# Dealing the 8 KB runs of a KV cache to the SBUF partitions in another order

## The chip, the cores and the metric

One core of one Trainium2 chip runs the kernel. The metric is the device time of one launch in microseconds (us). The core has five instruction queues: TensorE (PE, with its weight loads shown as PEld), VectorE (DVE), ScalarE (ACT), GpSimd (POOL) and SyncE (SP). SP computes nothing here; it issues nearly all transfers between DRAM and the on-chip memory SBUF, which has 128 partitions. 16 DMA engines carry the transfers out in packets; one packet is one contiguous run.

## The reference

One decode step of an attention block and a gated MLP side by side on the same normalised input, and the gradient of it for all inputs but one. All data are bf16.

```python
xn = _layernorm(x)                                   # x: [2, 1, 576]
q = (xn @ wq).reshape(B, Sq, 32, 128)                # 32 query heads, 16 KV heads
scores = einsum("bhqd,bhkd->bhqk", q, k) * 128**-0.5 # k_cache, v_cache: [2, 16, 4096, 128]
o = einsum("bhqk,bhkd->bhqd", softmax(scores), v)
out = x + o.reshape(B, Sq, 4096) @ wo + ((xn @ w_gate) * (xn @ w_up)) @ w_down
_out, _vjp = jax.vjp(_f, A_x, A_k_cache, A_v_cache, A_wq, A_wo, B_w_gate, B_w_up, B_w_down)
_grads = _vjp(grad_out)
```

The outputs are `out` and the gradients of `x`, both caches (each as large as the cache, 32 MB), `wq`, `wo` and the three MLP weights. There is one query position, so a cache is read once, and its gradient is an outer product that is written once. The sum over the 4096 keys doesn't depend on the order of the keys, as long as K, V and their gradients use the same order.

## The kernel before

The function is one long builder. Python generators (`load_kv`, `turn`, `softmax`, `dscore`, `contract`, `head_outer`, `put` and others) yield requests, and a planner (`Order`, lines 105 to 240) runs them against a table of costs and priorities and so writes down one fixed order of instructions for each engine. Nothing is scheduled on the chip: SP issues its transfers in the order written, and each waits for the semaphores of its data or buffer. The planner lets at most eight transfers of the hardware queue be in flight: an issue waits for the landing of the one eight places before it (line 186).

The work is cut into 16 steps: 8 groups of two KV heads, times 2 batch entries. For each step and each of the two heads:

- `load_kv` (lines 1108 to 1121) loads one K head and later one V head, 4096 x 128 elements or 1 MB each, into one of the 16 shared `big` tiles (128 partitions x 4096 elements). The load is issued at line 1117: `nc.sync.dma_start(kv_t[i][:], views[t][b, G * g + l])`. There are 64 such loads.
- `turn` (line 1175) transposes 32 x 32 blocks on DVE (the helper at line 464) into another `big` tile, and `score` (line 1228) multiplies on PE (line 1234). `softmax` and `dscore` follow.
- `contract` (line 1390) uses the loaded tile itself for the weighted sum over the keys (line 1407).
- `head_outer` (line 1244) forms the gradient of a K or V head with PE (line 1255), ACT or DVE copy it from PSUM into a `big` tile (helpers at lines 468 and 470), and `put` (lines 687 to 692) stores it through `oviews`. The store's issue is line 691. There are 64 such stores of 1 MB.

A head's 4096 keys lie in DRAM as 1 MB without a gap. `views` and `oviews` (lines 1105 and 1106) tell which keys go to which partition: partition p holds the 32 keys from 32p on, an 8 KB run. All code between load and store treats the position within a tile as the key's name, and nothing in it uses the key's place in DRAM.

Beside that, `load_w` (line 1123) brings the weights, `group_front`, `group_back` and `mlp` work on them, and the weight gradients leave through `put` too: `rows_outer` with 4,608-byte rows, `cols_store` and `wide_outer` with rows of 1 to 4 KB over 128 partitions, and `tail_outer` (line 808), which stores 64 rows of 1 KB from 64 partitions of a `tl` tile.

Of the kernel before, what the change touches and what calls it, by code (L numbers as in the profile page):

```python
# [13 lines left out]
P = 128  # L14
# [339 lines left out]
def kernel(  # L354
# [747 lines left out]
    wS = [[None] * 2 for _ in range(NS)]  # L1102
    bE = [[Event() for _ in range(2)] for _ in range(NS)]
    bS = [[None] * 2 for _ in range(NS)]
    views = [A.rearrange("b h (p c) d -> b h p (c d)", p=P) for A in (A_k_cache, A_v_cache)]
    oviews = [A.rearrange("b h (p c) d -> b h p (c d)", p=P) for A in (out_2, out_3)]

    def load_kv():
        n = 0
# [449 lines left out]
```

## Time and profile before

| | us |
|---|---|
| median of three runs | 478.5 (477.12 to 479.41) |
| the profiled execution | 480.7 |
| its span, first to last instruction | 478.9 |
| DVE busy | 369.2 |
| PE busy | 375.8 |
| ACT busy | 335.6 |

The profiled execution is one run; its span leaves 1.8 us of start and end around it. Each engine's busy time is a share of that span. A line of the profile such as "L691" is a line of the code. "out_dram<-big" is a store from a `big` tile, "big<-in_A_k_cache_dram" a load. The row of DMA tenths has 40 slices of 12 us, each with the mean busy share of the 16 DMA engines. The queue line gives packets, megabytes, and the time of the packets as a share of 16 engines' span. The chain is the work that ended last, followed back from the last instruction. A wait line tells who waited, for whom, and the total in us, the times and the longest. The granted clock of TensorE was 0.704 in the mean.

### The profile page before, as it was taken

What the parts mean: (1) busy time and instruction counts of PE and PEld (TensorE: products, weight loads), DVE (VectorE), ACT (ScalarE), POOL (GpSimd) and SP (SyncE); (2) the same over time, 40 slices, a digit from 0 to 9 for tenths busy, and PEclk for the clock granted to TensorE, in tenths of its full rate; (3) what the DMA queues carried; (4) which work ended last, traced back from release to release, by engine and by line L of the source; (5) the groups of instructions that cost most, each with busy time, mean ns of one, the idle gap of its engine ahead of it and who ended that gap; (6) DMA issues with size and microseconds to landing.
All of it is one profiled execution on the core that took longest, in us unless ns stands there. A gap on an engine that the chain in (4) does not pass through costs nothing.

```text
span 478.9 us, 15380 instructions
## 1 busy us (share of the span) xinstructions
PE 375.8 (78%) x6538; PEld 214.9 (45%) x6538; DVE 369.2 (77%) x708; ACT 335.6 (70%) x507; POOL 152.0 (32%) x208
## 2 busy tenths in 40 slices
PE   1668588989878877768878986599887769898894
PEld 1545353545554534446344453464444424444452
DVE  8788787867867976786956987889677958888781
ACT  3139659966787693833869875399776978897871
POOL 0440074343003643003434530032644556333000
PEclk9979676556766677885567595859656876656876
DMA  8999999999999999999999999999999999999994
GB/s 299 355 405 419 391 402 380 353 377 422 422 400 371 395 365 393 423 414 389 316 399 384 354 402 422 421 413 406 346 414 415 418 419 422 419 417 391 425 369 187
DMA packets 41925, 185.95 MB, mean 388 GB/s; under 512 B 3960, under 2 KB 13440, under 8 KB 25472
## 3 DMA queue, kind: packets, MB, share of 16 engines
q1 hardware_dynamic: 41848, 184.96, 98.3%
q8 instruction: 51, 0.84, 0.7%
q14 instruction: 18, 0.15, 0.1%
q10 hardware_dynamic: 8, 0.00, 0.0%
HBM read 92.48 MB, written 92.48 MB: 386 GB/s over the span
## 4 chain that ended last, share of the span: by engine, by line
DMA 46%; PE 25%; DVE 14%; ACT 8%; issue 3%; SPq 2%; POOL 1%; DVEq 0%; ACTq 0%; POOLq 0%
DMA out_dram<-big 18%; DMA big<-in_A_v_cache_dram 15%; DVE big L464 8%; ACT big L468 7%; PE ps_o L1255 4%; DMA big<-in_A_k_cache_dram 4%; PE ps_m L1234 4%; PE ps_m L1407 4%; PE ps_o L722 3%; DMA gu<-in_B_w_up_dram 3%; DMA ww<-in_A_wo_dram 3%; DMA big<-in_B_w_gate_dram 2%; DVE big L470 2%; PE ps_m L678 1%; PE ps_o L759 1%
## 5 line engine op out<-in xcount | busy, mean ns | idle before, releaser
L468 ACT CAST big<-ps_o 128x1024 bf16<-128x1024 f32 (+2 forms) x310 | 277.6, 958 | 47.6 <-PE ps_o L1255 18.9
L464 DVE STREAM_TRANSPOSE big<-big 128x1024 f32<-128x1024 f32 x146 | 175.9, 1224 | 29.7 <-DMA out_dram<-big 16.2
L1222 POOL TENSOR_TENSOR BD<-vr,mask 128x2048 bf16<-128x2048 bf16 x32 | 115.3, 3603 | 105.4 <-ACT vr L468 49.8
L470 DVE CAST big<-ps_o 128x1024 bf16<-128x1024 f32 (+2 forms) x68 | 74.2, 1093 | 16.4 <-PE ps_o L722 7.4
L1234 PE MATMUL ps_m<-big,W 128*32 128x128 bf16 x2048 | 59.9, 282 | 11.3 <-DVE cr L1359 2.6
L1234 PEld LDWEIGHTS <-W 128*32 128x32 bf16 x2048 | 46.7, 125 | 27.9 <-issue 25.7
L1255 PE MATMUL ps_o<-BD,dd 32*128 32x512 bf16 x256 | 45.8, 480 | 9.9 <-ACT big L468 7.9
L671 POOL COPY wt<-wm 64x128 bf16<-64x128 bf16 (+1 forms) x34 | 8.9, 261 | 138.2 <-DVE wm L664 119.5
L1255 PE MATMUL ps_o<-BD,pp 32*128 32x512 bf16 x256 | 48.2, 520 | 5.5 <-ACT big L468 4.0
L1199 POOL COPY W<-rep 32x16 bf16<-32x16 bf16 x128 | 24.5, 192 | 55.8 <-DVE rep L983 33.6
L464 DVE STREAM_TRANSPOSE big<-ww 128x1152 f32<-128x1152 f32 x25 | 34.0, 1359 | 7.7 <-DMA ww<-in_B_w_down_dram 3.5
L1407 PE MATMUL ps_m<-big,pp 128*32 128x512 bf16 x256 | 30.2, 547 | 3.8 <-DMA big<-in_A_v_cache_dram 3.3
L1255 PEld LDWEIGHTS <-dd 32*128 32x128 bf16 x256 | 12.2, 98 | 32.1 <-issue 27.6
L1407 PE MATMUL ps_m<-big,dd 128*32 128x512 bf16 x256 | 25.8, 491 | 0.4 <-DVE oT L1427 0.2
L1255 PEld LDWEIGHTS <-pp 32*128 32x128 bf16 x256 | 10.4, 97 | 28.1 <-issue 24.2
L872 PE MATMUL ps_m<-big,Wdy 128*128 128x128 bf16 x162 | 15.4, 269 | 4.8 <-DVE rz L1320 3.1
L722 PE MATMUL ps_o<-dyr,hb 32*32 32x288 bf16 x288 | 18.0, 382 | 0.2 <-ACT big L468 0.2
L759 PEld LDWEIGHTS <-xnr 32*128 32x128 bf16 x368 | 12.9, 116 | 10.8 <-issue 9.7
L722 PE MATMUL ps_o<-dyr,R 32*32 32x288 bf16 x256 | 16.2, 378 | 1.3 <-ACT big L468 0.9
L872 PEld LDWEIGHTS <-Wdy 128*128 128x128 bf16 x162 | 13.6, 121 | 6.8 <-issue 6.7
L759 PE MATMUL ps_o<-D,xnr 32*128 32x128 bf16 x256 | 13.0, 276 | 3.9 <-issue 2.2
L1308 ACT COPY mr<-m 1x128 f32<-1x128 f32 x16 | 4.7, 295 | 15.8 <-DVE m L1306 15.6
(205 smaller groups left out, 487.3 us busy)
## 6 DMA issues: line engine op xcount, KB each, us to landing
out_dram<-big SPq DMA_DIRECT2D x74, 1024.0 KB, 12.8
big<-in_A_k_cache_dram SPq DMA_DIRECT2D x32, 1024.0 KB, 12.7
big<-in_A_v_cache_dram SPq DMA_DIRECT2D x32, 1024.0 KB, 13.2
out_dram<-big SPq DMA_DIRECT2D x17, 576.0 KB, 10.7
ww<-in_B_w_down_dram SPq DMA_DIRECT2D x9, 576.0 KB, 13.5
ww<-in_A_wo_dram SPq DMA_DIRECT2D x8, 576.0 KB, 7.3
ww<-in_A_wq_dram SPq DMA_DIRECT2D x8, 512.0 KB, 8.0
big<-in_B_w_gate_dram SPq DMA_DIRECT2D x4, 1024.0 KB, 12.3
```

Source lines behind the costliest of these rows:

```text
L464: nc.vector.transpose(out, in_)
L468: nc.scalar.copy(out, in_)
L470: nc.vector.tensor_copy(out=out, in_=in_)
L671: nc.gpsimd.tensor_copy(view(Wt[:], 64 * h, 64, 0, [[dims[-1][1], n], [1, dims[-1][1]]]), view(Wm[:], 64 * h, 64, off, dims))
L722: nc.tensor.matmul(o[32 * q:32 * q + 32, aa, 0:HD2], lhsT=view(t, 32 * q, 32, 2 * A + aa, [[4, 32]]), rhs=dyr[32 * q:32 * q + 32, k * HD2: ...
L759: nc.tensor.matmul(o[:, aa, j * P:(j + 1) * P], lhsT=xnr[32 * a:32 * a + 32, dc * P:(dc + 1) * P], rhs=rhs(a), start=True, stop=True)
L872: nc.tensor.matmul(dh, lhsT=Wdy[:, e, 2 * k:2 * k + P], rhs=view(X[:], 0, P, 64 * k + e, [[D, FC], [2, 32]]), start=(k == 0 and e == 0), s ...
L1199: nc.gpsimd.tensor_copy(view(W_t[t][w][:], 32 * a, 32, 6 + 8 * a, [[G * WW, 4], [WW, G], [1, 2]]), view(rep_t[grp[g]["qs"]][:], 32 * a, 32 ...
L1222: nc.gpsimd.tensor_tensor(BD_t[i][:], view(vr_t[v][:], 0, P, 0, [[0, 16], [1, Dh]]), view(mask16[:], 0, P, 0, [[1, 16], [0, Dh]]), ALU.mult)
L1234: nc.tensor.matmul(sc[32 * cq:32 * cq + 32, :], lhsT=view(W[:], 0, P, (be * G + l) * WW + 6 - 4 * c2 - 2 * l, [[1, 32]]), rhs=view(X[:], 0 ...
L1255: nc.tensor.matmul(o[:, k, :], lhsT=pr2[32 * c4:32 * c4 + 32, :], rhs=BD[32 * c4:32 * c4 + 32, 8 * l + 4 * h2:8 * l + 4 * h2 + 4, :], star ...
L1407: nc.tensor.matmul(ct[32 * j:32 * j + 32, :], lhsT=view(rT, 0, P, 4 * c + 2 * l, [[1, 32]]), rhs=kv_t[kvS[s][t][l]][:, Dh * c:Dh * (c + 4) ...
```

## The change

Two lines change. The 128 runs of 8 KB of a head go to other partitions: before, partition p holds run p; after, partition 8e + j holds run 16j + e, for e from 0 to 15 and j from 0 to 7. Loads and gradient stores use the same rule, so the keys of a head are permuted alike everywhere.

```diff
-    views = [A.rearrange("b h (p c) d -> b h p (c d)", p=P) for A in (A_k_cache, A_v_cache)]
-    oviews = [A.rearrange("b h (p c) d -> b h p (c d)", p=P) for A in (out_2, out_3)]
+    views = [A.rearrange("b h (j e c) d -> b h e j (c d)", e=16, j=8) for A in (A_k_cache, A_v_cache)]
+    oviews = [A.rearrange("b h (j e c) d -> b h e j (c d)", e=16, j=8) for A in (out_2, out_3)]
```

The tile's side of the transfer stays 128 partitions of 8 KB; the DRAM side becomes 16 x 8 runs of 8 KB, with a step of 8 KB between the 16 and of 128 KB between the 8.

## The prediction

> **What bounds the kernel now.** I read the page's totals first, then the DMA queues, then the chain that ended last, then what SyncE (SP) waits for before its issues, and last the trace's single DMA packets. Totals and queues:
>
> ```profile
> span 478.9 us, 15380 instructions
> PE 375.8 (78%) x6538; PEld 214.9 (45%) x6538; DVE 369.2 (77%) x708; ACT 335.6 (70%) x507; POOL 152.0 (32%) x208
> ...
> DMA  8999999999999999999999999999999999999994
> ...
> DMA packets 41925, 185.95 MB, mean 388 GB/s; under 512 B 3960, under 2 KB 13440, under 8 KB 25472
> ...
> q1 hardware_dynamic: 41848, 184.96, 98.3%
> ```
>
> No compute engine is above 78%, but the 16 DMA engines are occupied in 38 of 40 slices, and SP's queue alone takes 98.3% of 16 engines' span. Of 478.9 us about 4 us are left in which an engine had no packet. So a change of packet time goes almost fully into the end, and a few tenths at an issue hardly do. The chain agrees:
>
> ```profile
> DMA 46%; PE 25%; DVE 14%; ACT 8%; issue 3%; SPq 2%; POOL 1%; DVEq 0%; ACTq 0%; POOLq 0%
> DMA out_dram<-big 18%; DMA big<-in_A_v_cache_dram 15%; DVE big L464 8%; ACT big L468 7%; PE ps_o L1255 4%; DMA big<-in_A_k_cache_dram 4%; PE ps_m L1234 4%; PE ps_m L1407 4%; PE ps_o L722 3%; DMA gu<-in_B_w_up_dram 3%; DMA ww<-in_A_wo_dram 3%; DMA big<-in_B_w_gate_dram 2%; DVE big L470 2%; PE ps_m L678 1%; PE ps_o L759 1%
> ```
>
> The DMAs on it are the ones that the change touches: stores from `big` and the two cache loads. The waits of SP's queue (total us, times, longest) and the issues themselves (ns min/median/max):
>
> ```profile
> SPq L691 <- ACT big L468: 82.6, 49, 7.7
> SPq L691 <- DVE big L470: 49.9, 17, 6.8
> SPq L1117 <- DMA out_dram<-big: 31.9, 13, 4.8
> ```
>
> ```profile
> L1117 SPq DMA_DIRECT2D big<-in_A_k_cache_dram x32: 327/372/1742, 0.7 to 404.2; - x32
> ```
>
> ```profile
> L691 SPq DMA_DIRECT2D out_dram<-tl x26: 472/507/1971, 34.3 to 469.6; - x26
> ```
>
> SP has slack: its 249 issues take 150 us in all, and a cache load lands 12.7 to 13.2 us after its issue, five transfers of 2.45 us deep.
>
> **The packets.** The trace holds length and size of each. Exactly 16,384 packets of SP's queue have 8,192 B, and they are the cache runs (64 loads and 64 stores of 128 runs): 1,024 for each engine. Their median is 309 ns, 88% lie at or under 313, the mean is 320.7. At 309 they are 1,024 x 0.309 = 316 us of each engine's 475. The excess of the mean is 1,024 x 11.7 ns = 12.0 us, no more. It sits in a few places. From 280 to 304 us, where cache loads and stores alternate, it is nearly absent (mean 312). From 265.6 to 267.1 us, at the start of a store that follows a store, most engines have two or three packets of 600 to 750 ns:
>
> ```profile
> 280.00:304.00 24.00, 16.58 (x361) 10.23 (x364) 18.78 (x35) 12.68 (x21) 2.50 (x11) 0.79 1.01 423
> 264.00:268.00 4.00, 4.00 (x78) 2.15 (x76) 3.24 (x5) 4.00 (x6) 3.60 (x1) 0.50 1.01 322
> ```
>
> The last two columns are DMA share and GB/s: full both times, at 423 and at 322.
>
> **The change, part by part.** No instruction is added or removed, and the order of every engine is the same; in the built program only the shapes of the 128 cache DMAs change: 128 rows on both sides become 16 x 8 rows on the DRAM side and 128 x 1 on the SBUF side. Bytes, run length and packet count stay. Keys are only permuted, alike in K, V and both gradients. Three terms follow.
>
> *DRAM side.* If the slow 8 KB packets come from where the engines stand in DRAM, the change can win up to all of the excess; bounds 0 and -12.0 us. A new clash is bounded by the SBUF term below. Most packets already run at 309, so I take 0 for the forecast and keep -12.0 for the range.
>
> *Issue.* An issue with a shape of its own for each side isn't in the trace. The nearest rows: 128-row issues 327 ns at least, 64-row ones 471. So 0 to +0.14 us each, x128 = 0 to 18 us of SP time. SP's waits (82.6 + 49.9 + 31.9 us in the three rows) and five transfers of depth hide it. Cover is gone only where the DMA engines run dry, as at 224 to 232 us (share 0.77): a handful of times 0.14 us, under 1 us, and at most 5 us if a dependency chain carries thirty of them. I take 0.
>
> *SBUF side.* The new leading count is 16, one for each engine, so the claim of the change (engine e at run 16j + e) means that engine e moves the eight neighbouring partitions 8e to 8e+7. Is that what it has now? The trace doesn't name partitions, but it shows that it matters which ones the engines hold. The transfers with 64 rows (line 812, `tl`) have 1 KB packets, and 46 ns is such a packet alone. From 228.6 to 230.1 us, when the queue had run dry and the engines were in step, two such stores ran: of 120 packets 44 took 50 ns or less and 60 took 66 to 88, often as twins (two at 228.743 us of 79 each, two at 228.77 of 74, two at 228.823 of 79). In the 1 KB stores from 460 to 469 us, nearly all with 128 rows, 1,043 of 1,080 took 50 or less. Half the partitions, and engines meet in pairs, each at about half pace. The first cache load, with all engines in step from 2.6 to 5.2 us, has 87 of 111 packets at 316 ns or less and one over 500: today's deal of 128 rows gives every engine a place of its own. If 64 partitions hold places for 8 engines, then 128 hold 16, and a different deal can put two engines on one.
>
> Price: bounded below by the row alone, 309 ns, so 0; above by the doubled row. 8 KB packets of exactly 606 ns occur 26 times (twice 309 less one fixed 12), so 1,024 x (606 - 309) = +304 us. Between these the overlap decides. Engines drift: the 16 landings of a cache DMA lie 3.4 us apart from first to last, the first ten within 0.73 us, two taken at random 0.75 us (medians over 128 DMAs). A stay of eight packets is 2.45 us, one of four 1.22. Two engines 0.25 us apart overlap for 0.90 or 0.80 of it, 0.75 apart for 0.69 or 0.39. A DMA lands with its last engine and at most eight are in flight, so the pair that is closest sets the pace; I take 0.80: 0.80 x 304 = +243 us.
>
> [...]
>
> **Sum.** The profiled execution took 480.7 us (span 478.9 and 1.8 around it). 480.7 + 0 + 0 + 243 = 723.7. It was 2.2 above the median of the runs, 478.5, so on the medians 721.5, **722 us**.
>
> **The rivals.** (1) *Faster: the DRAM order works and SBUF doesn't mind.* Place: the starts of stores while engines are in step. Price: of the 12.0 us of excess 9.9 lie in packets over 400 ns, and 2.9 of these in packets over 800 ns, starts after a dry queue; 9.9 - 2.9 = 7.0, and 478.5 - 7.0 = **471.5**. It decides if the cache packets keep 309 ns, that is if engines don't share places. For it: packets of 600 to 750 ns on most engines at once look like one shared target, and 16 neighbouring runs can't be the same one at any lag. Against it: 423 GB/s in the long stretches, with the old order.
>
> (2) *Nothing: the SBUF rows stay with their engines, or don't care, and DRAM doesn't either.* **478.5**, within 2.4. For it: the 309 of most packets looks like the engine's own pace. [...]
>
> (3) *Slightly slower:* the packets stay, but the longer issues (up to 0.14 us) reach the end where the queue is shallow, up to 5 us, or a new order meets in DRAM now and then: **483**.
>
> **How the numbers follow.** Forecast 0.58, because the twins and the clean first load speak for places and the new shape can't keep the old deal and do what it says; (1) 0.21; (2) 0.13; (3) 0.08. This kernel's measurement tells about 0.5% (2.4 us) from no change. So faster 0.21, same 0.13, slower 0.58 + 0.08 = 0.66. The cases lie far apart and both signs hold much. The forecast's own range is 600 (overlap 0.4: 478.5 + 122) to 770 (0.96). For 8 in 10 I must take in (1), (2) and (3): 468 (478.5 less 10.5 of the 12.0) to 770.
>
> **What would show it.** Right: 8 KB packets with a mean near 550 ns and many at 606, the DMA share still at 0.9 or more in nearly all slices at about 250 GB/s, cache DMAs landing some 20 us after issue, every compute engine at about two thirds of its present share, other sizes as before. Wrong for (1): 8 KB mean at 310 to 313 and no group of 600 ns. Wrong for (2): mean 321 as now. Issues of lines 691 and 1117 show the second term: 330 to 370 ns, or 470 and more. The prediction falls if the new deal still gives each engine its own eight partitions of one place, or if the twins of the 64-row stores come from DRAM and not from the partitions.

## The result, and the profile after

The changed kernel takes 574.1 us (median of four runs, 569.7 to 575.0) against 478.1 us (477.1 to 479.4) for the kernel before, measured together: a ratio of 1.199, interval 1.195 to 1.203. That is 96 us more. I had predicted 722 us. The direction was right, and the size was two and a half times too large.

The profiled execution took 575.0 us with a span of 573.2 us. From the totals, the slices and the queues of the changed kernel's page:

```profile
span 573.2 us, 15380 instructions
PE 394.5 (69%) x6538; PEld 222.5 (39%) x6538; DVE 370.8 (65%) x708; ACT 336.9 (59%) x507; POOL 152.4 (27%) x208
...
DMA  8999999999999999999999999999999999998996
GB/s 215 301 225 267 310 263 317 323 234 377 398 364 323 394 296 249 393 357 350 323 265 330 356 304 349 399 319 388 271 321 365 362 353 361 367 372 291 369 369 187
DMA packets 41925, 185.95 MB, mean 324 GB/s; under 512 B 3960, under 2 KB 13440, under 8 KB 25472
...
q1 hardware_dynamic: 41848, 184.96, 99.1%
```

The reader is to see three things. The packets and the bytes are exactly those of before, and the DMA engines are as full as before (99.1% of the span). So the engines don't stand idle longer: the same packets take longer, and the rate falls from 388 to 324 GB/s. The loss is uneven: slices of 215 to 270 GB/s stand beside slices of 390 to 400. The compute engines' busy times change little (DVE 369.2 to 370.8, PE 375.8 to 394.5 at a granted clock of 0.644 in place of 0.704); their shares fall, because the span is longer.

The chain that ended last has moved towards the transfers, from 46% to 67%:

```profile
DMA 67%; PE 15%; DVE 6%; ACT 5%; issue 2%; SPq 2%; POOL 1%; DVEq 0%; ACTq 0%; POOLq 0%
```

In the view of single lines, an issue of a cache load now takes at least 536 ns where it took 327 (columns: ns at least, median and at most, then the start of the first and of the last issue in us):

```profile
L1117 SPq DMA_DIRECT2D big<-in_A_k_cache_dram x32: 536/586/1891, 0.7 to 486.2; - x32
...
L1117 SPq DMA_DIRECT2D big<-in_A_v_cache_dram x32: 536/587/2025, 13.7 to 505.3; - x32
```

A K load lands 17.2 us after its issue (12.7 before). The time and the size of every packet in the trace tell where the 96 us are. Per DMA engine, all packets together took 474.6 us before and 572.1 us after, 97.6 us more:

| packets | mean before | mean after | per engine |
|---|---|---|---|
| 8,192 B, cache loads and stores, 1,024 per engine | 320.7 ns | 399.2 ns | +80.3 us |
| 2,048 B, weight loads, 288 | 100.0 | 121.3 | +6.1 |
| 1,024 B, loads and stores, 528 | 49.7 | 61.2 | +6.0 |
| 4,608 B, loads and stores, 272 | 197.2 | 207.8 | +2.9 |
| 512 B, weight loads, 64 | 27.5 | 42.7 | +1.0 |
| 4,096 B, stores only, 160 | 160.7 | 163.1 | +0.4 |

The median of the 8 KB packets is 309 ns in both kernels. What is new is a second group: about 130 packets took 540 to 640 ns before, about 2,900 after. It isn't there all the time either. In the windows view of the changed kernel (start and end in us, length, busy time of PE, PEld, DVE, ACT and POOL, granted clock, DMA share, GB/s):

```profile
0.00:64.00 64.00, 33.30 (x640) 21.36 (x640) 40.20 (x118) 24.37 (x41) 12.53 (x29) 0.83 0.99 250
136.00:160.00 24.00, 19.33 (x357) 11.71 (x358) 15.46 (x30) 13.36 (x21) 4.18 (x3) 0.67 1.02 407
```

The kernel before, in the same two windows:

```profile
0.00:64.00 64.00, 38.30 (x806) 25.57 (x806) 52.30 (x142) 30.21 (x51) 16.80 (x34) 0.85 0.99 376
136.00:160.00 24.00, 19.93 (x392) 12.46 (x381) 19.15 (x35) 17.61 (x30) 8.35 (x17) 0.64 1.01 388
```

With the same full DMA share, the changed kernel's first 64 us run at 250 GB/s and the 24 us from 136 at 407; the kernel before had 376 and 388. In the first window the cache transfers that land are loads; of the nine that begin to land in the second, six are stores.

### The profile page after: what moved, and what is told of

Its sections match the earlier page's. It is cut to its first block, busy times and chain, and to the rows that moved or that the text cites. A ratio compares the mean times of both kernels' runs of the same rounds, so it can differ in the third digit from the quotient of the medians.

```text
span 573.2 us, 15380 instructions
## 1 busy us (share of the span) xinstructions
PE 394.5 (69%) x6538; PEld 222.5 (39%) x6538; DVE 370.8 (65%) x708; ACT 336.9 (59%) x507; POOL 152.4 (27%) x208
## 3 DMA queue, kind: packets, MB, share of 16 engines
q1 hardware_dynamic: 41848, 184.96, 99.1%
## 4 chain that ended last, share of the span: by engine, by line
DMA 67%; PE 15%; DVE 6%; ACT 5%; issue 2%; SPq 2%; POOL 1%; DVEq 0%; ACTq 0%; POOLq 0%
DMA out_dram<-big 26%; DMA big<-in_A_v_cache_dram 21%; DMA gu<-in_B_w_up_dram 6%; DMA big<-in_A_k_cache_dram 5%; DMA ww<-in_A_wq_dram 4%; ACT big L468 4%; DVE big L464 3%; DMA ww<-in_A_wo_dram 3%; DMA ww<-in_B_w_down_dram 3%; PE ps_m L1234 2%; PE ps_m L1407 2%; PE ps_o L1255 2%; PE ps_o L722 2%; POOL BD L1222 1%; DVE big L470 1%
## 5 line engine op out<-in xcount | busy, mean ns | idle before, releaser
L1234 PE MATMUL ps_m<-big,W 128*32 128x128 bf16 x2048 | 62.8, 290 | 15.9 <-DVE cr L1359 6.1
L1234 PEld LDWEIGHTS <-W 128*32 128x32 bf16 x2048 | 48.5, 128 | 36.3 <-issue 34.7
L1255 PE MATMUL ps_o<-BD,pp 32*128 32x512 bf16 x256 | 49.6, 530 | 8.6 <-ACT big L468 4.2
L1255 PE MATMUL ps_o<-BD,dd 32*128 32x512 bf16 x256 | 47.6, 506 | 9.3 <-ACT big L468 6.9
L1407 PE MATMUL ps_m<-big,dd 128*32 128x512 bf16 x256 | 28.1, 526 | 1.0 <-issue 0.8
L1304 PE MATMUL ps_m<-identf,mx 128*1 128x128 f32 x16 | 5.4, 340 | 25.9 <-DVE mx L1296 25.6
L1255 PEld LDWEIGHTS <-pp 32*128 32x128 bf16 x256 | 10.2, 98 | 31.3 <-issue 27.5
L722 PE MATMUL ps_o<-dyr,R 32*32 32x288 bf16 x256 | 17.2, 401 | 2.0 <-ACT big L468 1.6
## 6 DMA issues: line engine op xcount, KB each, us to landing
big<-in_A_k_cache_dram SPq DMA_DIRECT2D x32, 1024.0 KB, 17.2
```

The source lines that it names most:

```text
L722: nc.tensor.matmul(o[32 * q:32 * q + 32, aa, 0:HD2], lhsT=view(t, 32 * q, 32, 2 * A + aa, [[4, 32]]), rhs=dyr[32 * q:32 * q + 32, k * HD2: ...
L1234: nc.tensor.matmul(sc[32 * cq:32 * cq + 32, :], lhsT=view(W[:], 0, P, (be * G + l) * WW + 6 - 4 * c2 - 2 * l, [[1, 32]]), rhs=view(X[:], 0 ...
L1255: nc.tensor.matmul(o[:, k, :], lhsT=pr2[32 * c4:32 * c4 + 32, :], rhs=BD[32 * c4:32 * c4 + 32, 8 * l + 4 * h2:8 * l + 4 * h2 + 4, :], star ...
L1407: nc.tensor.matmul(ct[32 * j:32 * j + 32, :], lhsT=view(rT, 0, P, 4 * c + 2 * l, [[1, 32]]), rhs=kv_t[kvS[s][t][l]][:, Dh * c:Dh * (c + 4) ...
```

## The experiments

The theory in all of them is that of the prediction: two DMA engines that want the same place in SBUF at the same moment take turns, and the new deal puts them there. It is an inference from times: no trace here names a place. The rivals are the order in DRAM, the longer issues, and a shape that is slow for an engine by itself.

**e1_loads: only the loads are dealt anew.**

```diff
-    views = [A.rearrange("b h (p c) d -> b h p (c d)", p=P) for A in (A_k_cache, A_v_cache)]
+    views = [A.rearrange("b h (j e c) d -> b h e j (c d)", e=16, j=8) for A in (A_k_cache, A_v_cache)]
```

> Only the 64 cache loads get the new deal; the stores keep the old one, so the gradients land in another order of keys. Theory A (places in SBUF: with the new deal an engine moves eight neighbouring partitions, and shares their places with another engine, each direction by itself): about half of the +96 us, 515 to 535 us; 8 KB packets of loads up to 606 ns, those of stores at 309; the weight loads, which write into SBUF too, slower as well, the 64-row stores not. Rival B (the engines meet in DRAM because 16 neighbouring runs are one target): about half as well if reads and writes are alike, but then only one of the two halves if not. Rival C (longer issues, 327 to 536 ns): 64 issues x 0.2 us = 13 us of SP time, nearly all hidden, so under 485 us.

Measured: 574.2 us (572.6 to 577.6), a ratio of 1.199 (1.192 to 1.206), mean of the 8 KB packets 403 ns. That is above the 515 to 535 us that I expected: the loads alone carry the whole loss.

**e2_stores: only the gradient stores are dealt anew** (the `oviews` line of the change, and not the `views` line).

> Only the 64 gradient stores get the new deal; the loads keep the old one, so the gradients land in another order of keys. Theory A: the other half, 515 to 535 us; 8 KB packets of stores up to 606 ns, loads of all sizes as before (512 B packets at 27 ns, 8 KB loads at 309). Rival B: as for the loads. Rival C: under 485 us.

Measured: 500.0 us (498.7 to 503.8), a ratio of 1.046 (1.039 to 1.053), mean of the 8 KB packets 335.8 ns, which is +15.5 us per engine of +17.1 for all packets. That is below the 515 to 535 us expected: stores cost something, a fifth of what loads cost, and beside the dealt loads it doesn't add up. Two causes were possible, the issues and the packets. The issue row of this kernel is nearly as long as that of the full change (343/552 ns at least and in the median, against 344/576; 332/344 before):

```profile
L691 SPq DMA_DIRECT2D out_dram<-big x96: 343/552/2276, 32.4 to 486.7; - x96
```

**e4_issue: the issues alone.** One line at the start of the kernel before turns a switch of the build off:

```diff
+    nc.dge_precook = False
```

> The kernel before with one switch of the build changed, so that every DMA issue of SP is expected to take the long way (470 to 540 ns where a 128-row issue took 327); all transfers, their shapes and their order stay. It asks where the 21 us of the stores-only kernel come from. Theory 'issue' (SP's 0.2 us more per store reach the end): this kernel, in which 249 issues are longer and not 64, is slower by as much or more, 495 to 510 us. Theory 'packets' (the stores' own packets, or what they do to the packets beside them): 478 to 483 us, mean of the 8 KB packets 321 ns as before.

Measured: 478.6 us against 478.3, a ratio of 1.0015 (0.9998 to 1.0032), mean of the 8 KB packets 318.8 ns. The issues did get longer:

```profile
L1117 SPq DMA_DIRECT2D big<-in_A_k_cache_dram x32: 471/552/1279, 0.7 to 401.2; - x32
...
L691 SPq DMA_DIRECT2D out_dram<-big x96: 471/504/3550, 32.7 to 467.4; - x96
```

Some 0.14 us more on each of the 128 issues of these two rows, and on the 32 of the V loads (472 ns at least), costs nothing that can be measured. In the stores-only kernel 64 issues grew by 0.21 us, less in all. So I put its 21 us down to the packets: they hold 17.1 of the 18.0 us by which the profiled span grew (478.9 to 496.9 us).

**m1_forms: the forms by themselves.** A kernel of transfers only, no two of which need each other: `run("load", form, 14)` and `run("store", form, 14)` for the old rows, the new deal, and a third form with the new shape but its 16 leading rows 80 KB apart in DRAM; then loads in two halves of 64 partitions.

```python
if form == "rows":
    return x.rearrange("(p c) d -> p (c d)", p=P)
if form == "deal":
    return x.rearrange("(j e c) d -> e j (c d)", e=16, j=8)
x = x.rearrange("(p c) d -> p (c d)", p=P)
return bass.AP(x.tensor, x.offset, [[40960, 16], [4096, 8], [1, 4096]])
```

> Transfers alone, no computing; of the outputs only part of one cache gradient is written, with cache data. Each stage starts when the one before has landed: 14 loads in the old deal, 14 in the new one, 14 in the shape of the new one but with each engine's eight runs contiguous in DRAM and the engines 80 KB apart; then 14 stores of each kind; then 10 heads loaded as two transfers of 64 rows. One transfer of 1 MB takes 2.45 us at 309 ns a packet. Theory A: old deal 309 ns, 34 to 37 us for the stage; new deal and the 80 KB form alike, 606 ns at the start of the stage, when the engines are in step, 45 to 70 us for the stage; the same for stores; the halves 500 to 606 ns. Rival B: the 80 KB form at 309 like the old deal, only the new deal slow, and the halves at 309.

The windows of this kernel, one inside each stage and two in the stage of dealt stores (the last two columns are DMA share and GB/s; only POOL is named, and it does nothing):

```profile
4.00:36.00 32.00, 0.00 (x0) 1.00 1.01 423
44.00:104.00 60.00, 0.00 (x0) 1.00 1.01 219
112.00:172.00 60.00, 0.00 (x0) 1.00 1.01 225
179.00:207.00 28.00, 0.00 (x0) 1.00 1.01 419
211.00:215.00 4.00, 0.00 (x0) 1.00 0.99 250
222.00:244.00 22.00, 0.00 (x0) 1.00 1.01 419
...
290.00:330.00 40.00, 0.00 (x0) 1.00 1.02 217
```

Loads: old deal 423 GB/s, new deal 219 (packets of 604 ns), new shape with another DRAM order 225, and halves of 64 partitions, whose DRAM order is the old one, 217. The other order in DRAM is worth 3% here (225 against 219); the halving comes without the new order (217) and stays with the other one (225). Stores: old 419, and the new deal 250 for some microseconds and then 419. The third form's stores, in a window left out here, ran at 420 GB/s. So my "each direction by itself" doesn't hold evenly: stores were slow only at their start and recovered by themselves; loads didn't in 60 us.

**e5_near and e6_wide: the same loss without the change, and its absence with the same issues.** The kernel before, each cache load issued as two transfers of 64 partitions, first of neighbours, then of every second partition (of the second kernel only the inner line is shown):

```diff
-                    nc.sync.dma_start(kv_t[i][:], views[t][b, G * g + l])
+                    for h in range(2):
+                        nc.sync.dma_start(kv_t[i][64 * h:64 * h + 64, :], views[t][b, G * g + l][64 * h:64 * h + 64, :])
```

```diff
+                        nc.sync.dma_start(kv_t[i][h:P:2, :], views[t][b, G * g + l][h:P:2, :])
```

> The kernel before, all of it computed, with each cache load issued as two transfers of 64 neighbouring partitions; rows, partitions, DRAM addresses and the number of packets stay as they were, stores too. Theory 'places in SBUF': loads meet in pairs as in the changed kernel, 540 to 590 us, mean of the 8 KB packets 380 to 410 ns. Rival 'order in DRAM': nothing has changed there, 478 to 485 us (64 more issues of 0.47 us), mean 321 ns.

> The kernel before, all of it computed, with each cache load issued as two transfers of 64 partitions again, but of every second partition and every second row, not of neighbours. Issues, packets, rows and the partition of every row are those of the near halves, and in DRAM it is every second run of 8 KB. Theory 'places in SBUF': in the trace of the transfers alone such halves ran at 309 ns, so 478 to 485 us and a mean near 321 ns. Rival 'a load in two transfers costs it' (64 more issues, 8 rows fewer per engine and transfer, two semaphores): 560 to 590 us, like the near halves.

Measured: neighbours 579.8 us (574.3 to 583.2), ratio 1.209 (1.204 to 1.214); every second partition 480.2 us (478.0 to 482.2), ratio 1.004 (1.0015 to 1.0065). The 8 KB packets take 405.9 ns in the mean in the one and 319.4 in the other. The rates by slice on the page of the neighbours and on that of every second partition:

```profile
GB/s 206 294 221 247 306 277 319 316 241 367 335 286 367 338 348 235 350 399 341 350 264 281 420 276 361 319 343 344 345 273 366 280 414 332 301 385 385 405 409 230
```

```profile
GB/s 290 359 402 420 382 418 405 366 390 422 420 401 360 417 354 411 423 409 369 331 392 417 353 407 423 418 400 401 332 392 412 418 418 421 419 424 400 424 385 195
```

This pair is the strongest evidence of the study. Neighbours leave the deal in DRAM untouched, and yet their first slices (206, 294, 221, 247) are nearly those of the change (215, 301, 225, 267). Both kernels have the same number of issues, packets and bytes, and the same partition for every row. Only which rows, and so which partitions, go together in one transfer differs, and 100 us with it.

**m3_places: how few engines are enough.** Transfers only: loads of 128 rows, of halves and quarters, of the new shape cut to its first 4 and first 8 rows of 16, then stores.

```python
x = A_k_cache[heads[2 * i % 32]].rearrange("(j e c) d -> e j (c d)", e=16, j=8)
nc.sync.dma_start(big[i % 8][0:8 * e, :], x[0:e])        # e = 4, then 8
```

> Transfers alone, no computation (all outputs but part of one are left out). Stages in order: loads of 128 rows (8 of 1 MB); loads in halves of 64 neighbouring partitions (16 x 0.5 MB); in halves of every second partition (16 x 0.5 MB); in quarters of 32 partitions (24 x 0.25 MB); loads in the new shape with only 4 leading rows (32 partitions) and with 8 (64 partitions), 8 each; then stores of 128 rows, of 64 neighbouring and of every second partition. Theory 'shared places' (writes of two engines into one place of SBUF take turns): 64 neighbours near 604 ns for an 8 KB packet; 4 leading rows near 309 ns if 4 engines carry them, since they share nothing, and 8 leading rows near 604 ns; all stores near 315 ns. Rival 'slow shape' (an engine that writes neighbouring partitions by a list of this shape is slow by itself): 4 leading rows near 604 ns like 16. Every second partition is open: 309 ns if the halves then reach all places one engine each, 604 ns if every engine's four rows lie as in the new deal.

```profile
28.00:60.00 32.00, 0.00 (x0) 1.00 1.02 219
72.00:84.00 12.00, 0.00 (x0) 1.00 1.01 425
92.00:114.00 22.00, 0.00 (x0) 1.00 1.03 220
118.50:121.50 3.00, 0.00 (x0) 1.00 0.26 109
123.00:133.00 10.00, 0.00 (x0) 1.00 0.51 131
141.00:149.00 8.00, 0.00 (x0) 1.00 0.50 148
...
181.00:207.00 26.00, 0.00 (x0) 1.00 0.89 266
218.00:230.00 12.00, 0.00 (x0) 1.00 0.96 399
```

In order: loads of 64 neighbours 219 GB/s, of every second partition 425, of 32 neighbours 220. Then four engines alone (DMA share 0.26, a quarter of 16) move 109 GB/s, and all 40 of their 8 KB packets in this window take 309 to 318 ns. As soon as four more run beside them (share 0.51), eight engines move 131, hardly more than four did, with a median of 542 ns; later it gets better (148). So the shape isn't slow for an engine by itself; it is slow in company. I had put 8 rows at a steady 604 ns, and that was wrong: the engines' landings of one such load lay 14 to 22 us apart, and the 8 loads of 4 rows ahead of them were, by my estimate from the 309 ns, 8 x 8 x 0.309 = 20 us of work for four engines only. The last two rows are stores: 64 neighbours 266 GB/s, every second partition 399. Reading from 64 neighbouring partitions is slow too.

Every second partition, which I had left open, needs a word. If the 16 engines took four neighbouring rows each of such a half, every engine would stay within the eight partitions that I give it in the new deal, and by the theory the half would have been slow. It ran at 425 GB/s. So either the rows of a half are dealt to the engines in some other way, or the places aren't quite what I take them for; no trace here names the engine of a row.

**m2_lag: engines held back by hand.** Dealt loads, three times interrupted by small copies from DRAM to DRAM that were meant to give some engines extra packets: four copies of 4 rows of 8 KB; four of 8 rows; four of 4 rows and four of 12. The engine numbers in the expectation are my naming: no trace here shows which engine takes which row.

> Loads alone in the new deal, no computing, no output but a few copied rows. One stage of 14 loads; then three stages of 3 loads, a handicap, 12 loads. The handicap: four DRAM-to-DRAM copies of 4 rows of 8 KB, which keep engines 0 to 3 busy for some four packets; the same with 8 rows (engines 0 to 7); with 4 rows and then 12 rows (engines 0 to 3 twice, 4 to 11 once). [...] Rival B (16 neighbouring runs are one target in DRAM): the handicap of 8 engines helps as much as that of 4 or more, and no stage splits in halves.

Measured: 217 GB/s before, then 222, 220 and 231. The 16 landings of a load, 0.2 to 0.6 us from first to last before, lay at most 1.7 us apart afterwards. My guess had been half of the engines at 309 ns after the first handicap and nearly all after the third; it took for granted which engines meet, which no run shows, and neither came. So lags of up to 1.7 us didn't free the loads, and the simple picture in which half a transfer's lag (1.2 us) is enough for a pair isn't confirmed.

**m4_mixed: loads and stores in turn.** Transfers only, 16 pairs of each combination: `mixed("rows", "rows", 16)`, then old loads with dealt stores, dealt loads with old stores, and both dealt.

> Transfers alone, no computation (all outputs but part of one are left out). After 8 loads four stages of 16 load-and-store pairs of 1 MB, alternating: old/old, old loads with new stores, new loads with old stores, new/new. Theory 'only writes into SBUF meet, and only while two engines are in loads at once': old/old 309 to 325 ns mean (about 80 us for the 32 transfers); old loads with new stores the same within 5 ns; new loads with old stores between 388 ns (the share of 0.53 that the whole kernel shows: 309 + 0.53 x 295 / 2) and 457 ns (loads fully doubled), so 99 to 117 us; new/new the same. Rival 'stores meet too once loads run beside them': old loads with new stores at 336 ns or more, the mean of the stores-only kernel.

```profile
26.00:82.00 56.00, 0.00 (x0) 1.00 1.01 427
104.00:116.00 12.00, 0.00 (x0) 1.00 1.01 410
136.00:176.00 40.00, 0.00 (x0) 1.00 1.01 427
186.00:256.00 70.00, 0.00 (x0) 1.00 1.01 428
266.00:332.00 66.00, 0.00 (x0) 1.00 1.01 428
```

A plain miss: I expected 388 to 457 ns for dealt loads beside stores, and they ran at 309, 428 GB/s, from their first packet to the last. The dealt stores ahead of them had lost a little (410 GB/s), and meanwhile the engines had moved apart: the landings of one transfer lay up to 0.8 us apart in the first stage, drifted to 3.2 us in the second, and stayed 3.2 to 3.4 us apart in the dealt loads and after. With these lags the new deal cost nothing: 428 GB/s against the 427 of old loads and old stores.

**m5_runs: from one step, and longer rows.** The same dealt loads and old stores, now starting with all engines in step; 1, 2 and 4 of each in turn, then 12 loads in a row; last, bursts of two old loads and two stores of the same tiles, between which the queue runs dry.

```python
groups("deal", "rows", 1, 12)
groups("deal", "rows", 2, 7)
groups("deal", "rows", 4, 5)
for i in range(12):
    one("load", "deal")
bursts("rows", 7)
bursts("deal", 7)
```

> Transfers alone, no computation (all outputs but part of two are left out). Loads have the new shape, stores the old one, in the order: 12 times load, store; 7 times two loads, two stores; 5 times four and four; 12 loads in a row; then, with the queue drained each time, 7 bursts of two old loads and two stores of the same tiles, with old stores and with new ones. Theory 'turns' (two engines slow each other only while both are in loads, and their lag of a DMA lets them miss each other where loads and stores alternate): near 309 ns in the first part, more the longer the row of loads, so 309 to 350 with two, 350 to 457 with four (457: loads doubled, stores not), 604 with 12. In the bursts new stores run slower than old ones, since each drained queue puts the engines back in step: 10 to 100 ns more on the mean of loads and stores, which would be the 21 us of the stores-only kernel. Rival 'order in DRAM' (a store beside the loads made room in DRAM): no dependence on the length of the row, and bursts alike within 5 ns.

```profile
26.00:50.00 24.00, 0.00 (x0) 1.00 1.01 307
76.00:100.00 24.00, 0.00 (x0) 1.00 1.00 325
126.00:150.00 24.00, 0.00 (x0) 1.00 1.01 337
...
190.00:280.00 90.00, 0.00 (x0) 1.00 1.01 419
289.00:311.00 22.00, 0.00 (x0) 1.00 1.01 384
324.00:400.00 76.00, 0.00 (x0) 1.00 0.92 361
406.00:504.00 98.00, 0.00 (x0) 1.00 0.92 292
```

The length of the row, which I had made the deciding thing, came out the other way round: single loads in turn with stores are the slowest (307 GB/s in the first window, 432 ns in the mean of that part), four in a row run at 419, and 12 in a row, which took 604 ns in m1_forms, took 339 here (384 GB/s). The parts ran in this one order, so length and time since the start aren't separated within this kernel. But single dealt loads in turn with old stores ran at 428 GB/s in m4_mixed, behind stages in which the engines had drifted apart, and at 307 here, from a start in step. So the history of the engines decided far more here than the row.

The size of the spread alone isn't it. The landings of one load lay 0.7 us apart at 27 us and already 6.9 us apart at 71 us, while the 8 KB packets of the first part still took 432 ns; only about 150 us after the start in step, with the spread still near 7 us, were they back at 309. Which engines are apart, and by how much, may matter; the traces don't tell it. The bursts show the other half: with the queue run dry each time, dealt stores and old loads ran at 292 GB/s (410 ns), old stores and old loads at 361 (334 ns). The stores-only kernel may lose its time in the same way, at new starts in step; that wasn't looked for in its trace.

**Does the kernel itself follow this?** In the trace of the changed kernel I took, for each of the 64 cache loads, how far the first ten of its 16 landings lie apart, and the mean of the 8 KB packets that start within 4 us of its first landing:

| first ten landings within | loads | mean 8 KB packet |
|---|---|---|
| under 0.7 us | 10 | 582 ns |
| 0.7 to 1.4 | 4 | 492 |
| 1.4 to 2.1 | 9 | 429 |
| 2.1 to 2.8 | 7 | 380 |
| 2.8 to 3.5 | 10 | 429 |
| 3.5 to 5.0 | 17 | 418 |
| over 5.0 | 7 | 359 |

Loads whose engines are close are slow loads here too; from 1.4 us on the mean hardly follows the spread. Those that land in the first 57 us, with ten landings within 0.5 to 0.6 us, fill the window of 250 GB/s above. The two that land from 123 to 130 us lay within 0.3 to 0.4 us again, and the 8 KB packets from 120 to 132 us took 581 ns; those that land from 239 to 260 us lay 4 to 5 us apart, with packets of 359 to 364 ns from 240 to 264 us. What brings the engines back into step in the kernel (a dry queue, a mix of sizes) wasn't isolated, and the 8 KB packets from 140 to 148 us, when three dealt stores landed with their engines in step within 0.3 us, took 327 ns in the mean: stores in step were hardly slowed there.

## Why the prediction was right in kind and wrong in size

- **What bounds the kernel:** right. The DMA engines are full in both kernels, and a change of packet time went into the end almost whole: +97.6 us of packets per engine, +94.3 of span.
- **DRAM side, taken at 0:** nothing speaks against it. In m1_forms another DRAM order changed the new shape's rate from 219 to 225 GB/s, and the old order runs at 423. A kernel with the old deal in SBUF and the new order in DRAM wasn't tried, so a part of the 12.0 us may still lie there.
- **Issue term, taken at 0:** the value was right and its upper bound was too low. The issue grew by 0.21 us (327 to 536 ns at least), not by at most 0.14. That longer issues are hidden is shown for 0.14 us on 160 of them, 22 us in all (e4_issue), and inferred for 0.21 us on 128, 27 us in all.
- **SBUF side:** that it matters which partitions are written together is shown, in the whole kernel (579.8 us in e5_near against 480.2 in e6_wide) and in transfers alone (219 GB/s against 425 in m3_places, 217 against 423 in m1_forms). The doubled price held too: 604 ns in m1_forms for the 606 of the prediction (its "fixed 12" stands in no row; 46 ns for 1 KB and 84 for 2 KB, the medians before, leave 8). That engines meet in fixed pairs isn't shown, nor how many places 64 partitions hold, and m2_lag speaks against the simplest form of such pairs (217 GB/s before the lags, 220 to 231 after). The twins were thinner evidence than the prediction made of them. Stores of 64 neighbours did run slower than those of every second partition (266 and 399 GB/s), but in the kernel before, 20 of the 23 transfers of 64 rows from `tl` that were issued before 450 us landed among 1 KB packets of 46 to 48 ns in the mean; only those issued at 80, 226 and 228 us stood among packets of 63 to 65. So that trace already showed that these small stores are mostly not slowed.
- **The step that failed** is the size of this term: "so the pair that is closest sets the pace; I take 0.80: 0.80 x 304 = +243 us". Both factors were too large. First, 304 us counts all 1,024 packets of an engine, but only the 512 of the loads stayed slow (604 ns for 60 us in m1_forms): 512 x (604 - 309) = 151 us. Stores started slow and recovered within about 10 us (250, then 419 GB/s in m1_forms); beside the dealt loads they added nothing measurable (e1_loads, 574.2 us, equals the whole change, 574.1). Second, the overlap was 80.3/151 = 0.53, not 0.80, if all of the 8 KB packets' loss is put down to the loads (the trace doesn't tell a packet's direction). Over the first 1,024 of the 16,384 packets, the loads at the start, it was 16.2 us of 8 x 8 x 0.295 = 18.9, so 0.86; over the other 56 loads 64 us of 132, so 0.49. The 0.80 rests on a stay of four or eight packets at one place, which no run shows; what the runs showed in its place is the 0.53. And I treated the lag between engines as given by the kernel before, and it isn't: in m5_runs dealt loads in turn with stores went from 432 ns to 309 in some 150 us, while only the rows grew from one transfer to four.
- **"Other sizes as before":** wrong, and worth 16.4 us (the table above). The weight loads write into SBUF beside the dealt loads and are slowed with them: the 2 KB and 512 B packets grew by 6.1 and 1.0 us per engine, by 0.6 and 0.2 where only the stores were dealt anew (e2_stores). The 4 KB packets, which are only stores, hardly are (+0.4). So +243 became 80 + 16 = +96.
- **What was to be seen:** the mean of the 8 KB packets was 399 ns and not 550, the rate 324 GB/s and not 250 (250 holds for the first 64 us), a load lands 17 us after its issue and not 20.
- **The rivals:** faster (471.5), nothing (478.5) and slightly slower (483) are refuted by the ratio.

Loads of 32 and of 64 neighbouring partitions ran at 220 and 219 GB/s, loads of every second partition, 64 as well, at 425 (m3_places). How many partitions a transfer fills doesn't settle it: the new deal fills all 128 and still ran at 219 (m1_forms). What the runs show is that it matters which partitions are written together, and what the engines did before: single dealt loads in turn with old stores ran at 307 GB/s from a start in step (m5_runs) and at 428 behind stages in which the engines had drifted apart (m4_mixed). Which engine meets which stays open, and so does why a queue of loads alone never moved apart while stores and mixtures did.

## What to carry to other kernels

A DMA that fills all 128 partitions can still load at half the rate (219 GB/s against 423) when only the order changes in which its rows go to the partitions: look at the packet lengths for a second group at twice the first, before arguing about DRAM. Such a loss depends on what the engines did before: it was largest in a queue of loads alone (219 GB/s for 60 us in m1_forms), absent or fading in two mixtures of loads and stores (428 GB/s in m4_mixed; 307 at first and 419 later in m5_runs), and still cost the whole kernel 96 us. When a resource can be shared in time, price the two directions separately, and treat the overlap as something that the transfers will change themselves.

## What the runs showed of the hardware that I had not expected

- Loads in the new deal ran at 219 GB/s (604 ns for 8 KB) as long as only loads were queued, for 60 us without a change (m1_forms); the same loads took 339 ns in the mean behind a mixture with stores that had spread the landings of one load to 7 or 8 us (m5_runs).
- Stores in the new deal recovered from 250 to 419 GB/s within about 10 us (m1_forms).
- Eight engines in the new deal moved 131 GB/s, where four of them alone had moved 109 (m3_places).
- An issue of a dealt cache transfer, whose two sides have different shapes, took at least 536 to 538 ns on SP; one of equal 128-row shapes took 327 to 332 in the kernel before. Issues of 471 ns in place of these 327 to 332 made no difference to the end (e4_issue: ratio 1.0015, 0.9998 to 1.0032).
